# A table of places for preparation, constants and second stage of a fused block-sparse attention and long-convolution kernel

## The chip, the cores and the metric

One Trainium2 chip, one core. The metric is device time in microseconds (us), the median of several runs. The engines are PE (TensorE: matrix products; PEld its weight loads), DVE (VectorE), ACT (ScalarE), POOL (GpSimd) and SP (SyncE, which here only issues DMAs). Each works through its own queue in order and waits for semaphores of the others.

## What is computed

For 4 batches and 8 heads of 768 positions and 64 dimensions, causal attention over the best blocks: each query scores the means of the 12 key blocks of 64, keeps the top three and its own block, and attends to these alone. The heads side by side give x (4 x 768 x 512), which goes through a gated long convolution.

```
k_rep = k.reshape(B, H, n_blocks, 64, D).mean(axis=3)
gate = where(causal, einsum('bhsd,bhnd->bhsn', q, k_rep), -1e9)
mask = (top 3 blocks of gate, or own block) & causal
attn = softmax(where(mask, scale * q @ k.T, -1e9)) @ v
x = heads of attn side by side
x1, x2, x3 = split(x @ w_proj, 3)
x2c = irfft(rfft(x2, axis=1) * rfft(filter_fft, axis=0), axis=1)
out = (x1 * x2c * x3) @ w_out
```

## The kernel before, in words

**Pairs, groups, slots.** Two heads are a pair p (16 pairs, four in a batch). Each head's causal triangle is cut into three groups (`groups`, L390). A slot n is one group of one head: 96 slots, six a pair, 24 a batch. Pair p's slots begin at n0 = 6p. A slot (the loop at L700) issues, in program order: `scores(n+1)` (L400, three products into one of two PSUM tiles `sps`, tag `sc`), `exponentials(n)` (L412, one ACT instruction of 896 columns, then a causal cut on POOL), `flush()` (L600, DMAs and other steps put into `late`), the steps of `early[n]`, one step of the second stage, the constants of `fills[n]`, `products(n-1)` (L423, seven products of the exponentials with V into the one PSUM tile `o`; after a head's last group DVE divides into `xnat`, L445 and L446), more steps of the second stage, and the steps of `bank[n]`. The order written is the order in which each engine executes.

**Preparation of a pair** runs some ten slots ahead. `load` (L74) brings k, q, v. `prep_k` (L289) turns half a pair's k on PE (`turned_pair`, L282), casts it on ACT (L298) and sums its blocks on DVE (L301); at the second half two DMAs send it to KA and KB (L307). `prep_q` (L325) turns q, casts it to TQ (L333, ACT), keeps the rest in `ql` (L335, DVE) and sends the second head to QB (L339). `prep_kr` (L314) forms block means on POOL, `prep_gate` (L341) is sixteen small products, `prep_mask` (L354) ten maxima and two DVE operations, `prep_turn` (L367) turns the mask on PE and copies it (two direct copies for pairs 0 and 1; for later pairs one ACT copy to `m16` and two DMAs from SP). `prep_v` (L310) casts v on POOL. The loop at L647 gives each pair the same slots relative to n0, with exceptions for pairs 1 and 2.

**Second stage** (`hyena`, L478), a batch behind the attention. `turn_x` (L459) or a transposing DMA (L455) brings x to `xT`, `fold` (L471, DVE) makes sums and differences `xf`. Then six `x2` (P steps), six `fft` (F), eight `gates` (X, two PSUM tiles each), four `inverse` (I) and six `output` (O). The step's name in the change carries its numbers: X12 is `gates(dc=2, hf=1)`, F10 is `fft(j=0, which=1)`. `final` (L522) multiplies gate and inverse into `yT` on POOL (in the tail the second half on DVE, L529). A list gives the order, and a credit per slot (costs of 0.65 to 1.28 a step, L703 to L729) says when the next step is issued. In the last batch (`spread` false) the steps run after the slots, with their PSUM in the two `sps` tiles (L481).

**PSUM.** Tag `one` has three tiles in rotation, which kt, qt, g, mt, xt, and in the slots x2p, xx, x1p, x3p, ye, yo, op share; `o` has one.

**Prologue** (L606 to L630): constants, preparation of pair 0, the sine products of the transform's constants, warm products (`warm`, L89: products of a zero tile, 512 columns each, whose result nobody reads), the first scores. **Tail** (L730 to L748): the outputs of batch 2 that are left, warm products, `turn_x`, two gates, `fold`, and the last batch's list.

Of the kernel before, what the change touches and what calls it, by code (L numbers as in the profile page):

```python
# [14 lines left out]
AX = mybir.AxisListType  # L15


@with_exitstack
def kernel(
# [10 lines left out]
    nc = tc.nc  # L30
# [58 lines left out]
    def warm(n):  # L89
        t = ps.tile([P, 512], FP32, name="warm", tag="o", bufs=1)  # L90
        for i in range(n):
            nc.tensor.matmul(t, lhsT=zeros[:, 0:P], rhs=zeros, start=True, stop=True,  # L92
                             skip_group_check=True)

    warm(3)
# [25 lines left out]
    def sine_products(i):  # L121
        if i != 1:
# [3 lines left out]
                         skip_group_check=True)  # L126
        ka = hy.tile([P, F], FP32, name="dft_ka", tag=f"t{i % 2 + 1}", bufs=3)
# [9 lines left out]
    def sine_rest(i):  # L137
        pr, kw = sine.pop(i)
        nc.tensor.matmul(pr, lhsT=idn, rhs=kw, start=False, stop=True, skip_group_check=True)
        nc.scalar.activation(FS[:, i, :], pr, AF.Sin, bias=0.0, scale=TWO_PI / S2)  # L140
# [4 lines left out]
    warm(3)  # L145
# [24 lines left out]
    TQ = [const.tile([P, S], fp, name=f"TQ{i}") for i in range(2)]  # L170
# [118 lines left out]
    def prep_k(p, t):  # L289
        kn = nats["k", p]  # L290
        kh = KH[p % 2]
        if t == 0:
            state["krs", p] = small.tile([P, NB], FP32, name="krs", tag="krs")
        krs = state["krs", p]
        kt = turned_pair("kt", kn, t)

        def cast():
            nc.scalar.copy(kh[:, F * t:F * (t + 1)], kt)  # L298

        def sums():  # L300
            nc.vector.tensor_reduce(out=krs[:, 6 * t:6 * t + 6],  # L301
                                    in_=kt.rearrange("p (n j) -> p n j", j=64),
                                    axis=AX.X, op=ALU.add)
        cast()
        sums()
        if t == 1:
            late.append(lambda: (nc.sync.dma_start(KA[p % 2][0:D, :], kh[0:D, :]),  # L307
                                 nc.sync.dma_start(KB[p % 3][0:D, :], kh[D:P, :])))
# [16 lines left out]
    def prep_q(p, t):  # L325
        qn = nats["q", p]
        tq = TQ[p % 2]
        if t == 0:
            state["ql", p] = hp.tile([P, S], fp, name="ql", tag="ql")
        ql = state["ql", p]  # L330
        qt = turned_pair("qt", qn, t)
        cols = slice(F * t, F * (t + 1))
        nc.scalar.activation(tq[:, cols], qt, AF.Copy, bias=0.0, scale=QS)  # L333
# [4 lines left out]
        if t == 1:  # L338
            late.append(lambda: nc.sync.dma_start(QB[p % 2][0:D, :], tq[D:P, :]))  # L339

    def prep_gate(p):  # L341
        tq, ql, kr = TQ[p % 2], state.pop(("ql", p)), state.pop(("kr", p))
# [24 lines left out]
    def prep_turn(p):  # L367
        mn, tq, qb = MN[p % 2], TQ[p % 2], QB[p % 2]
        mt = one("mt", (P, SC, P), fp)
        for c in range(SC):  # L370
            nc.tensor.transpose(mt[:, c, :], mn[:, c, :], id16)  # L371
        if p < 2:
            flat = mt.rearrange("p c s -> p (c s)")
# [7 lines left out]
        else:  # L381
            m16 = hp.tile([P, S], fp, name="m16", tag="m16")
            nc.scalar.activation(m16[64:108, :], mt[64:108].rearrange("p c s -> p (c s)"),  # L383
                                 AF.Copy, bias=0.0, scale=MQ)
            late.append(lambda: (nc.sync.dma_start(tq[64:64 + NB, :], m16[64:64 + NB, :]),
                                 nc.sync.dma_start(qb[64:64 + NB, :], m16[96:96 + NB, :])))
# [13 lines left out]
    def scores(n):  # L400
# [3 lines left out]
        qq = (QB if h else TQ)[p % 2]  # L404
# [20 lines left out]
    def products(n):  # L425
# [7 lines left out]
        first = g == 0  # L433
        for kc, q0, q1, col in groups[g][0]:
# [5 lines left out]
        if g == NS - 1:  # L440
# [8 lines left out]
            if h == 1:  # L449
# [3 lines left out]
                xT, xf = xTs[b], xTs["f", b]  # L453
                if p >= DC and dc < DC - 1:
                    late.append(lambda: nc.sync.dma_start_transpose(  # L455
                        xT[:, dc, :].rearrange("p (c s) -> p c s", s=P),
                        xn.rearrange("p c s -> p (c s)")))
# [20 lines left out]
    def hyena(b, spread):  # L478
# [8 lines left out]
        def x2(eo, i):  # L487
# [9 lines left out]
            (nc.scalar.copy if eo == 0 or not spread else nc.vector.tensor_copy)(st["x2"][:, eo, i, :], pa)  # L497
# [4 lines left out]
        def fft(j, which):  # L502
# [12 lines left out]
            else:  # L515
# [4 lines left out]
                nc.gpsimd.tensor_add(PQ[:, 1, j, :], tb, t4)  # L520
# [11 lines left out]
        def inverse(dc):  # L532
# [11 lines left out]
            yy = hy.tile([P, 2, F], FP32, name="yy", tag="yy", bufs=DC)  # L544
# [33 lines left out]
        x2s = [(0.85, lambda i=i, e=e: x2(e, i)) for e in range(2) for i in range(HC)]  # L578
        X = lambda dc, hf: (1.28, lambda: gates(dc, hf))
        Fh = lambda j, w: (0.65, lambda: fft(j, w))  # L580
        I = lambda dc: (0.96, lambda: inverse(dc))
        O = [(0.85, lambda i=i: output(i)) for i in range(SC)]
        if spread:
            steps = x2s + [X(0, 0), Fh(0, 0), Fh(0, 1), X(1, 0), Fh(1, 0), Fh(1, 1), X(2, 0),
                           Fh(2, 0), Fh(2, 1), X(3, 0), X(0, 1),
                           I(0), X(1, 1), I(1), X(2, 1), I(2), X(3, 1), I(3)] + O
        else:
            steps = [X(0, 0), X(1, 0)] + x2s[:4] + [
# [28 lines left out]
    for i in range(HC):  # L617
        sine_rest(i)
# [160 lines left out]
```

## Time and profile before

| | |
|---|---|
| time, median of 3 runs | 272.51 us (271.26 to 272.61) |
| the profiled execution's own time | 272.46 us |
| its span, first to last instruction | 270.7 us |
| mean granted TensorE clock | 0.979 |
| HBM read, written | 24.64 MB, 6.29 MB |

The profile is one execution. A row of the timeline is: start, duration (of the whole group if several), engine, line, operation, tiles written and read with their shape, count, and in brackets the idle time of the engine before it with what ended it. A row of the stages is: the stretch and its length, then for each engine the busy time and the count of instructions, the clock that PE was granted, the share of the 16 DMA engines (over 1 means that transfers overlap on an engine), and GB/s. A row of the waits is: who waited for whom, us in total, times, longest. In a row of groups the last numbers are busy us and mean ns of one.

### The profile page before, as it was taken

The page shows a single profiled execution, that of the slowest core. Times are in us where ns is not written, and L with a number is a line of the kernel's source. Part 1 is how long each engine was busy: PE and PEld are TensorE (multiplying, and loading weights), DVE is VectorE, ACT ScalarE, POOL GpSimd, SP SyncE. Part 2 cuts the span into 40 slices and gives each one's busy share as a digit, 9 for nine tenths or more (in the row PEclk, how much of TensorE's full clock was granted, in tenths as well). Part 3 has the DMA queues.
Part 4 walks back from the last instruction along what each step waited for, and adds up shares of the span by engine and source line. Part 5 has one row for each costly group of instructions (what it writes and reads, how often), then busy time and mean ns, then how long its engine had stood idle before and what let it go on. Part 6 is the DMA issues. An engine that isn't in the chain of part 4 may idle for free.

```text
span 270.7 us, 6236 instructions
## 1 busy us (share of the span) xinstructions
PE 242.0 (89%) x2228; PEld 150.3 (56%) x2228; DVE 179.1 (66%) x550; ACT 171.4 (63%) x275; POOL 140.9 (52%) x260
## 2 busy tenths in 40 slices
PE   7696869996999999989999999899999989897874
PEld 3365735565665667655656676566655654443431
DVE  3568658889477988654569885725698663256680
ACT  4567766774767577769764777797756756342333
POOL 7513342689635778653236876714277872006540
PEclk9999979997699999999999999999999999999999
DMA  8997977889797855677665467767241044200006
GB/s 162 209 153 208 245 205 140 157 162 212 128 190 159 155 124 131 125 210 232 150 134 121 106 150 105 190 212 195 59 93 37 1 33 155 77 2 0 0 0 232
DMA packets 93654, 36.29 MB, mean 134 GB/s; under 512 B 84292, under 2 KB 89784, under 8 KB 93624
## 3 DMA queue, kind: packets, MB, share of 16 engines
q1 hardware_dynamic: 91368, 33.81, 54.9%
q0 software_dynamic: 2256, 2.10, 5.9%
q8 instruction: 17, 0.28, 0.5%
q14 instruction: 13, 0.11, 0.2%
HBM read 24.64 MB, written 6.29 MB: 114 GB/s over the span
## 4 chain that ended last, share of the span: by engine, by line
PE 58%; DVE 15%; ACT 10%; POOL 6%; issue 4%; DMA 3%; SPq 1%; POOLq 0%; DVEq 0%; ACTq 0%
PE sps L407 8%; PE x2p L495 7%; PE op L572 6%; PE o L437 5%; PE x3p L560 5%; ACT ex L416 5%; PE x1p L557 4%; PE mt L371 2%; PE kt L285 2%; PE qt L285 2%; PE warm L92 2%; PE sps L557 2%; DVE xnat L446 2%; PE sps L560 2%; PE g L350 2%
## 5 line engine op out<-in xcount | busy, mean ns | idle before, releaser
L416 ACT ACTIVATE ex<-sps 128x896 f16<-128x896 f32 x96 | 88.3, 926 | 3.3 <-PE sps L407 3.0
L419 POOL TENSOR_SCALAR_AFFINE_SELECT ex<-ex 128x256 f16<-128x256 f16 x96 | 40.4, 424 | 82.6 <-ACT ex L416 78.3
L437 PEld LDWEIGHTS <-ex 128*128 128x128 f16 x672 | 32.7, 99 | 26.3 <-DVE xnat L446 11.6
L437 PE MATMUL o<-V,ex 128*128 128x65 f16 x672 | 37.5, 196 | 5.8 <-DVE xnat L446 4.4
L407 PE MATMUL sps<-QB,KB 76*128 76x512 f16 (+1 forms) x144 | 27.0, 297 | 3.7 <-ACT ex L416 3.6
L407 PE MATMUL sps<-TQ,KA 76*128 76x512 f16 (+1 forms) x144 | 27.4, 302 | 1.9 <-DMA QB<-m 1.3
L518 POOL TENSOR_TENSOR PQ<-ta 128x512 f16<-128x512 f32 x12 | 15.2, 1270 | 23.8 <-DVE ta L517 23.8
L572 PE MATMUL op<-wo,yT 128*128 128x512 f16 x96 | 24.2, 379 | 3.0 <-POOL yT L527 3.0
L301 DVE TENSOR_REDUCE krs<-kt 128x6 f32<-128x384 f32 x32 | 17.5, 553 | 13.5 <-ACT KH L298 13.3
L495 PE MATMUL x2p<-wp,xf 128*128 128x512 f16 x96 | 24.3, 379 | 0.8 <-DVE xf L474 0.8
L298 ACT CAST KH<-kt 128x384 f16<-128x384 f32 x32 | 15.2, 481 | 13.9 <-PE kt L285 12.6
L333 ACT ACTIVATE TQ<-qt 128x384 f16<-128x384 f32 x32 | 15.7, 495 | 12.3 <-PE qt L285 12.1
L335 DVE SCALAR_TENSOR_TENSOR ql<-qt,TQ 128x256 f16<-128x256 f32 (+1 forms) x32 | 15.5, 485 | 11.7 <-ACT TQ L333 11.6
L565 DVE TENSOR_TENSOR gg<-x1sb,x3p 128x384 f32<-128x384 f16 x24 | 13.2, 551 | 12.7 <-ACT x1sb L563 7.9
L527 POOL TENSOR_TENSOR yT<-gg,yy 128x384 f16<-128x384 f32 x16 | 15.9, 997 | 10.4 <-DVE yy L545 10.3
L575 ACT COPY osb<-op 128x512 f32<-128x512 f32 x24 | 14.1, 587 | 10.8 <-PE op L572 9.2
L560 PE MATMUL x3p<-xT,wp 128*128 128x384 f16 x96 | 19.6, 326 | 0.5 <-DVE yy L546 0.5
L407 PEld LDWEIGHTS <-KB 76*128 76x128 f16 x144 | 13.6, 100 | 11.0 <-issue 5.6
L557 PE MATMUL x1p<-xT,wp 128*128 128x384 f16 x96 | 19.5, 326 | 0.0
L383 ACT ACTIVATE m<-mt 44x768 f16<-44x768 f16 x14 | 11.3, 805 | 12.6 <-PE mt L371 12.6
L446 DVE TENSOR_TENSOR xnat<-o,rc 128x384 f16<-128x384 f32 x32 | 17.8, 558 | 1.1
L359 DVE MAX8 m<-g 128x8 f32<-128x12 f32 x160 | 13.9, 161 | 6.8 <-PE g L350 6.8
(155 smaller groups left out, 498.0 us busy)
## 6 DMA issues: line engine op xcount, KB each, us to landing
q_nat<-in_q_dram SPq DMA_DIRECT2D x32, 192.0 KB
k_nat<-in_k_dram SPq DMA_DIRECT2D x32, 192.0 KB
v_nat<-in_v_dram SPq DMA_DIRECT2D x32, 192.0 KB
out_dram<-osb SPq DMA_DIRECT2D x24, 256.0 KB
QB<-TQ SPq DMA_DIRECT2D x16, 96.0 KB
KA<-KH SPq DMA_DIRECT2D x16, 96.0 KB
KB<-KH SPq DMA_DIRECT2D x16, 96.0 KB
wp<-in_moe_w_proj_dram POOLq DMA_DIRECT2D x12, 128.0 KB, 3.8
```

The costliest lines, as they stand in the source:

```text
L301: nc.vector.tensor_reduce(out=krs[:, 6 * t:6 * t + 6], in_=kt.rearrange("p (n j) -> p n j", j=64), axis=AX.X, op=ALU.add)
L333: nc.scalar.activation(tq[:, cols], qt, AF.Copy, bias=0.0, scale=QS)
L407: nc.tensor.matmul(t[:, col:col + q1 - q0], lhsT=kk[0:64 + NB, P * kc:P * (kc + 1)], rhs=qq[0:64 + NB, q0:q1], start=True, stop=True, skip ...
L416: nc.scalar.activation(ex, t[:, 0:W], AF.Exp, bias=0.0, scale=EXPS)
L419: nc.gpsimd.affine_select(out=tri, in_=tri, compare_op=ALU.is_ge, fill=0.0, base=0, pattern=[[0, 2], [1, P]], channel_multiplier=-1)
L437: nc.tensor.matmul(o[:, qc, :], lhsT=ex[:, c0:c0 + P], rhs=V16[p % 3][:, kc, h, 0:65], start=first, stop=False, skip_group_check=True)
L446: nc.vector.tensor_tensor(xn[:, :, D * h:D * (h + 1)], o[:, :, 0:D], rc.to_broadcast([P, SC, D]), op=ALU.mult)
L495: nc.tensor.matmul(pa, lhsT=xf[:, eo, dc, P * i:P * (i + 1)], rhs=wp[:, dc, Dm:2 * Dm], start=(dc == 0), stop=(dc == DC - 1))
L527: nc.gpsimd.tensor_mul(st["yT"][:, dc, 0:F], g, yy[:, 0, :])
L557: nc.tensor.matmul(x1p, lhsT=wp[:, d2, dsl], rhs=xT[:, d2, hs], start=(d2 == 0), stop=(d2 == DC - 1))
L560: nc.tensor.matmul(x3p, lhsT=wp[:, d2, 2 * Dm + P * dc:2 * Dm + P * (dc + 1)], rhs=xT[:, d2, hs], start=(d2 == 0), stop=(d2 == DC - 1))
L572: nc.tensor.matmul(op, lhsT=st["yT"][:, cc, P * i:P * (i + 1)], rhs=wo[:, cc, :], start=(cc == 0), stop=(cc == DC - 1))
```

## The change

All orders move into one table, `ORDER`. Each slot has seven places: 0 before `scores(n+1)`, 1 after the exponentials and before `flush`, 2 to 4 after it and before `products(n-1)`, 5 and 6 behind the products. A time is 7 x slot + place; a pair's times count from its n0, and are given for p modulo 4, or for a pair by itself. The preparation is split into steps with a time each: turn, cast and sums of k; turn, copy and rest of q; each DMA of its own; gate; maxima; turn, copy and DMA of the mask. The second stage's steps have a time in the table `mid` (two batches) or `last`, and the tail a list. `zeros` puts products of a zero tile, 256 columns, ahead of `products(n)` of the slots named; they add zero to `o`.

Besides: TQ has three buffers instead of two; masks of pairs from 2 on turn and copy five of six blocks, the first is cleared once; `yy` has three buffers instead of four; warm products in the prologue have 128 columns; the sine products are issued without ACT's step between them and their second half ahead of the gate; in the tail the fold stands ahead of the gates, and one of the additions into PQ is on DVE. A second way to turn q (`cast_q`, `split_q`, `send_q`) is there for pairs from `turned` = 16 on, which is none.

```diff
+ORDER = {
+    "ldk:0": -120, "ldq:0": -84, "ldv:0": -61, "k0:0": -77, "k1:0": -64, "kc0:0": -76, "ks0:0": -76,
+    "kc1:0": -62, "ks1:0": -64, "kd:0": -61, "q0:0": -57, "q1:0": -53, "qc0:0": -57, "qr0:0": -57,
+    "qc1:0": -50, "qr1:0": -50, "qd:0": -45, "kr:0": -54, "g:0": -43, "m:0": -39, "mt:0": -29,
+    "mc:0": -26, "md:0": -26, "v:0": -23, "x:0": 52, "f:0": 69, "ldk:1": -118, "ldq:1": -93,
+    "ldv:1": -57, "k0:1": -77, "k1:1": -71, "kc0:1": -76, "ks0:1": -76, "kc1:1": -64, "ks1:1": -61,
...
+    "ldv:2": -54, ... "kd:2": -51, "q0:2": -59, "q1:2": -50, "qc0:2": -52, "qr0:2": -51,
...
+    "wp20": 156, "wp21": 177, "wp22": 195, "wp23": 215,
+    "w0": 8, "w1": 12, "w2": 0, "w3": 2, "w4": 14, "w5": 0, "turned": 16,
+    "mid": [("P00", 30), ("P01", 31), ("P02", 38), ("P10", 43), ("P12", 47), ("P11", 50),
+        ("F00", 57), ("X00", 57), ("F10", 73), ("F01", 79), ("X01", 82), ("F11", 87), ("X03",
+        89), ("F02", 94), ("F12", 99), ("X11", 103), ("X02", 106), ("I1", 114), ("X10", 120),
+        ("I0", 130), ("I3", 130), ("I2", 136), ("X13", 151), ("X12", 158), ("O0", 163), ("O4",
+        171), ("O3", 177), ("O5", 178), ("O1", 185), ("O2", 194)],
+    "last": [("P00", 31), ... ("I3", 146), ("X12", 147), ("O1", 153), ("O0",
+        157), ("O4", 158), ("O3", 164), ("O2", 167)],
+    "tail": ["rO5", "x", "w2", "w0", "f", "X00", "X01", "P00", "P02", "P01", "P10", "F02",
+        "P11", "F00", "F01", "P12", "F10", "w4", "w1", "F11", "X03", "F12", "X10", "w2", "X11",
+        "X02", "I0", "X12", "I1", "I3", "w2", "w0", "I2", "w1", "X13", "O0", "w1", "O5", "O3",
+        "O1", "O4", "O2"],
+    "dve": ["P10", "P11", "P12"],
+    "zeros": {31: 1, 16: 1, 19: 1, 9: 4, 33: 3, 8: 2, 22: 1, 24: 1, 17: 3, 21: 2, 20: 1, 5: 3,
+        12: 1, 6: 1},
+}
...
+    def turn_k(p, t):
+        if t == 0:
+            state["krs", p] = small.tile([P, NB], FP32, name="krs", tag="krs")
+        state["kt", p, t] = turned_pair("kt", nats["k", p], t), 2
+
+    def cast_k(p, t):
+        nc.scalar.copy(KH[p % 2][:, F * t:F * (t + 1)], taken("kt", p, t))
...
+    def send_mask(p):
+        nc.sync.dma_start(TQ[p % 3][64:64 + NB, :], M16[p % 2][64:64 + NB, :])
+        nc.sync.dma_start(QB[p % 2][64:64 + NB, :], M16[p % 2][96:96 + NB, :])
...
+        for i in range(ORDER["zeros"].get(n, 0)):
+            nc.tensor.matmul(o.rearrange("p c d -> p (c d)")[:, 0:256], lhsT=zeros[:, 0:P],
+                             rhs=zeros[:, 0:256], start=first, stop=False, skip_group_check=True)
+            first = False
...
-                nc.gpsimd.tensor_add(PQ[:, 1, j, :], tb, t4)
+                (nc.vector if j == HC - 1 and not spread else nc.gpsimd).tensor_add(
+                    PQ[:, 1, j, :], tb, t4)
...
+    warm(ORDER["w3"])
     prep_kr(0)
     prep_gate(0)
     prep_mask(0)
-    for i in range(HC):
-        sine_rest(i)
-    nc.scalar.preload_act_table_set("natural_log_exp_and_others")
     mask_rows()
     for p, w in ((2, "k"), (1, "v"), (2, "q")):
         load(p, w)
-    warm(4)
-    prep_turn(0)
-    warm(2)
+    warm(ORDER["w4"])
+    turn_mask(0)
+    copy_mask(0)
...
     for n in range(slots):
+        def do(*places):
+            for i in places:
+                for f in work[n][i]:
+                    f()
+        do(0)
         if n + 1 < slots:
             scores(n + 1)
         exponentials(n)
+        do(1)
         flush()
+        do(2, 3, 4)
         if n:
             products(n - 1)
+        do(5, 6)
```

In `tail`, "rO5" is the one output of batch 2 that is left, "x" the turn of the last pair, "f" its fold, and "w2" two warm products of 512 columns.

More of the change, by code (lines that the diff above doesn't have):

```diff
@@ L144 @@
         sine_products(i)
-    warm(3)
+    for i in range(HC):
+        sine_rounded(i)
     idn = const.tile([P, P], fp, name="idn")
@@ L633, in buffer_rows @@
         nc.sync.dma_start(t[64:64 + NB, :], erow)
[L636 to L652 removed]
+    per = slots // B
@@ L699 @@
-    credit = 0.0
-    for n in range(slots):
-        b, m = divmod(n, per)
+        for i in range(3):
+            once[f"wp{i}{dc}"] = lambda dc=dc, i=i: load_wp(i, dc)
+    for name, f in once.items():
+        at(ORDER[name], f)
+    for b in range(1, B):
+        steps = hyena(b - 1, True)
+        for name, time in ORDER["last" if b == B - 1 else "mid"]:
+            at(7 * per * b + time, steps.pop(name))
+        rest = steps
+    for n in range(slots):
+        def do(*places):
[3 more added lines that the diff above has]
+        do(0)
```

307 lines of the change are left out of this document (154 added, 153 removed), and 31 rows, old and new, of the table ORDER.

## The prediction

> **What bounds the kernel now.** I read the page's head first, then the busy time of each engine by stage (columns: PE, PEld, DVE, ACT, POOL busy, granted clock, DMA share, GB/s). The cuts are the first exponential, the slots of the four batches (24 slots each), and the tail after the last exponential.
>
> ```profile
> span 270.7 us, 6236 instructions
> PE 242.0 (89%) x2228; PEld 150.3 (56%) x2228; DVE 179.1 (66%) x550; ACT 171.4 (63%) x275; POOL 140.9 (52%) x260
> ...
> 0.00:16.70 16.70, 12.70 (x56) 6.24 (x57) 7.74 (x49) 7.47 (x14) 8.86 (x30) 1.00 1.14 192
> 16.70:62.00 45.30, 37.76 (x441) 26.26 (x440) 34.96 (x121) 33.34 (x52) 22.29 (x51) 0.96 0.82 178
> 62.00:118.10 56.10, 52.88 (x533) 35.23 (x533) 41.99 (x125) 37.82 (x61) 38.85 (x69) 0.94 0.79 155
> 118.10:173.70 55.60, 53.36 (x543) 34.68 (x540) 38.66 (x120) 40.32 (x67) 30.69 (x56) 1.00 0.65 150
> 173.70:226.60 52.90, 50.56 (x480) 31.13 (x477) 34.77 (x100) 36.65 (x59) 28.38 (x47) 1.00 0.41 97
> 226.60:270.70 44.10, 34.72 (x190) 16.70 (x188) 20.94 (x37) 15.75 (x30) 11.87 (x11) 0.99 0.17 65
> ```
>
> The mean of 89% hides four regimes. From 62 to 226.6 us the tensor engine is the bound: idle 3.2, 2.2 and 2.3 us in the three stages, so an order can win little there. The first batch leaves PE idle 7.5 of 45.3 us. The tail leaves 9.4 of 44.1. Before 16.7 us no attention slot runs, and the DMA engines are full (share above 1). Gain has to come from the front, the first batch and the tail. A slot lasts 55.60/24 = 2.3 us.
>
> **The change part by part.** The sum goes against the profiled execution's own time, 272.46 us (span 270.7 and 1.8 around it); the median of 272.51 is the same within 0.05.
>
> *1. Prologue.* The warm products (products of a zero tile that only keep PE going) shrink from 512 to 128 columns, the sine products go ahead of the gate, the mask's turn follows the gate and 14 warm products.
>
> ```profile
> 4.46 1.46 PE L92 MATMUL warm<-zeros 128*128 128x512 f16 x3
> ...
> 5.71 1.49 PE L285 MATMUL qt<-id,q_nat 128*128 128x128 f32 x6
> ...
> 12.16 0.22 DVE L365 TENSOR_TENSOR MN<-lt,ownm 128x120 f16<-128x120 f16 x1
> 12.43 1.91 PE L92 MATMUL warm<-zeros 128*128 128x512 f16 x4
> 14.13 0.85 PE L371 MATMUL mt<-id,MN 128*128 128x128 f16 x6
> 15.02 0.56 DVE L377 TENSOR_SCALAR TQ<-mt 12x768 f16<-12x768 f16 x1 [2.64 <-PE mt L371]
> 15.72 1.62 PE L407 MATMUL sps<-TQ,KA 76*128 76x512 f16 x6
> ...
> 16.66 0.92 ACT L416 ACTIVATE ex<-sps 128x896 f16<-128x896 f32 x1 [2.14 <-PE sps L407]
> ```
>
> The mask is ready at 12.38 and its turn starts at 14.13: four warm products of about 0.43 us stand between, 1.7 us on the path that sets the first exponential. In the table the 14 small ones follow the gate directly: 14 x 0.43/4 = 1.5 us, from about 10.8 to 12.3, so they lie beside the maxima. The first warm products also end earlier (12 x 0.11 = 1.3 us after the sine products, which no longer wait for ACT between them), so the turn of q can leave up to 0.8 us sooner. At most 1.7 + 0.8 = 2.5, at least 0. What is late next is k: the DMA that puts its cast into KA queues behind ten loads of 192 KB, 1.97 MB at some 217 GB/s, 9 us, with DMA full:
>
> ```profile
> 7.20:10.65 3.45, 1.87 (x19) 1.35 (x19) 2.56 (x7) 1.45 (x3) 2.87 (x8) 1.00 1.39 219
> 10.65:14.06 3.41, 2.83 (x17) 1.07 (x14) 1.37 (x12) 2.18 (x4) 0.41 (x1) 1.00 1.22 200
> ```
>
> By this estimate k cannot be there long before 13, and scores not long before 13.5, so I take **-2.0**.
>
> *2. Zero products, 25 of 256 columns, in fourteen slots from 6 to 34.* They aim at the clock. Stretches just before and in the two drops:
>
> ```profile
> 34.20:37.70 3.50, 1.66 (x17) 1.04 (x17) 3.13 (x9) 2.99 (x5) 2.43 (x7) 0.99 0.69 202
> 37.70:41.10 3.40, 3.40 (x30) 1.84 (x29) 1.06 (x2) 0.92 (x1) 0.75 (x2) 0.51 0.82 198
> ...
> 58.10:61.50 3.40, 3.10 (x29) 1.84 (x29) 2.85 (x8) 2.63 (x6) 3.08 (x5) 1.00 0.46 105
> 61.50:65.00 3.50, 1.88 (x31) 1.45 (x30) 3.16 (x15) 1.41 (x3) 3.33 (x8) 0.99 1.01 224
> 65.00:68.40 3.40, 2.95 (x26) 2.12 (x24) 3.21 (x8) 1.66 (x3) 3.38 (x6) 0.50 1.23 224
> 68.40:71.80 3.40, 3.39 (x27) 2.61 (x25) 1.83 (x6) 2.66 (x4) 1.64 (x5) 0.50 0.60 80
> ```
>
> Each drop follows a stretch with PE busy about half (1.66 and 1.88 of 3.5 us). The six zeros of slots 9 and 10 add 6 x 0.107 = 0.64 us to the first; 0.107 is half of 0.215 a product, which the 21 products of the tail's last row (part 4) give. Those of slots 20 to 25 add some 0.7 to the second. In the drops PE was busy 3.40 + 2.95 + 3.39 = 9.74 us at half speed: full speed saves at most 4.9. If nothing is saved and no zero falls in a wait, they cost 25 x 0.107 = 2.7. DVE is as full as PE in 65.00:68.40, so half of the saving stays behind it: -2.4, and of the zeros 0.4 on the path, since most fall where PE idles: **-2.0**.
>
> The Trainium skill, "TensorE: Matmul & The Clock Gate", section "Why this matters for your kernels", asks only that no PE idle gap exceed about 3 us, since one idle window lowers the clock. This trace disagrees: the clock fell after stretches with 17 and 31 products in 3.5 us. By the Trainium skill's page nothing would be there to hold, and the sum would lose this term (a rival below).
>
> *3. Slots.* The tables `mid` and `last` keep the work per slot and move the inverse ahead: in `mid` the last I stands at 136 (slot 19) and the first O at 163 (slot 23). Before, O(0) followed I(3) by one slot and waited for POOL's yT:
>
> ```profile
> PE op L572 <- POOL yT L527: 3.0, 4, 0.9
> ...
> 117.22 0.39 PE L572 MATMUL op<-wo,yT 128*128 128x512 f16 x1 [0.83 <-POOL yT L527]
> ...
> 122.53 0.50 PE L371 MATMUL mt<-id,MN 128*128 128x128 f16 x6
> ```
>
> Two of the four waits go: -1.7. In `last`, O1 (153) still follows I3 (146) by a slot: its wait stays. Masks of pairs 2 to 15 turn five blocks instead of six: 14 x about 0.055 = -0.8; the ACT copy shortens too, where ACT has room (63%). Against it, the load wp2 of block 3 is issued on POOL at 215 (slot 30, before: 29) and the first gates need it at slot 32:
>
> ```profile
> wp<-in_moe_w_proj_dram POOLq DMA_DIRECT2D x12, 128.0 KB, 3.8
> ...
> 81.26 0.65 PE x1p L557 x4
> ```
>
> Ten places of seven per slot are 1.4 x 2.3 = 3.3 us for a landing of 3.8 behind POOL's own waits; all of PE's queue stands behind the gates. Between 0 and 2 us; I take +0.5. DMA issues keep their order on SP but for neighbours (v's loads ahead of KA and KB in every fourth pair), whose users come six slots later: 0, with cover of some 14 us; were it gone, a load's 0.9 us. Holding casts and sums apart from the turns: 0, its other end is the slower rival. Slots: **-2.0** (bounds -4 and +12).
>
> *4. Tail.*
>
> ```profile
> 228.15 1.89 PE L572 MATMUL op<-wo,yT 128*128 128x512 f16 x8
> ...
> 228.59 0.56 DVE L446 TENSOR_TENSOR xnat<-o,rc 128x384 f16<-128x384 f32 x1
> ...
> 230.31 0.50 PE L467 MATMUL xt<-id,xnat 128*128 128x128 f16 x6
> 230.65 1.03 PE L92 MATMUL warm<-zeros 128*128 128x512 f16 x4
> ...
> 235.77 2.98 PE L495 MATMUL x2p<-wp,xf 128*128 128x512 f16 x13 [0.85 <-DVE xf L474]
> ...
> 255.69 1.06 DVE L529 TENSOR_TENSOR yT<-gg,yy 128x384 f16<-128x384 f32 x1
> ...
> 257.73 0.66 PE L537 MATMUL sps<-IC,PQ 128*128 128x384 f16 x3 [0.87 <-DVE yy L546]
> ...
> 259.69 0.82 PE L557 MATMUL sps<-xT,wp 128*128 128x384 f16 x4 [0.80 <-DVE yy L546]
> ...
> 262.25 4.71 PE L572 MATMUL op<-wo,yT 128*128 128x512 f16 x21 [0.44 <-POOL yT L527]
> ```
>
> The last row gives a product of 512 columns: 4.71 us for 21, about 0.215 apart beside the last one's drain. xnat is ready at 229.15, but its turn waits behind two outputs until 230.31. With one output left (rO5) it can go at 229.2: -1.1; the other output moves into the slots, where a wait covers half of its 0.86: +0.4. Two warm products fewer: -0.2 beside that. The fold now precedes the gates on DVE, so the 0.85 us wait of the first x2 goes: -0.85. With X12 and X13 between the inverses, two waits of 0.8 are half covered: -0.8. One PQ add moves from POOL to DVE, unseen there:
>
> ```profile
> L519 DVE TENSOR_TENSOR tb<-xx,Asb 128x512 f32<-128x512 f32 x6 | 4.1, 681 | 0.0
> ```
>
> Between 0.7 (this row) and 1.3 (yT's 1.0 us scaled from 384 to 512); half of 0.9 delays what follows: +0.5. The 11 warm products, 11 x 0.215 = 2.4 us, fit the 9.4 us idle: 0, without that cover 2.4. **-2.0** (bounds -5 and +2).
>
> Sum: 272.46 - 2.0 - 2.0 - 2.0 - 2.0 = 264.5 us.
>
> **The rivals.**
> *Data sets the front* (268.5). DMA's share of 1.14 before and 0.82 in the first batch speaks for it: slots that start sooner wait for k, q and the filter, and terms 1 and 2 vanish: 264.5 + 4.0. Against it: in 16.70:62.00 DMA still has a fifth free.
> *The zeros do not hold the clock* (266.9): the drop has another cause than PE's share, or its window moves with the start; 264.5 + 2.4. That is also what the rule of the Trainium skill's page on TensorE gives.
> *More idle closes* (257.5). PE idles 7.5 + 3.2 + 2.2 + 2.3 = 15.3 us in the slots; if the 300 separate places close half, 5.5 us go beyond what term 3 took, and 1.5 in the tail. Against it: DVE's 34.96 of 45.30 us.
> *Banks held longer: slower* (276.5). All turns, gates and hyena steps share three PSUM banks (tag `one`). The table releases them later: g at -43 and its maxima at -39, q's turn at -59 and its rest at -51, k's at -71 and its sums at -61. A step that needs two banks then stops PE. The precedent:
>
> ```profile
> PE g L344 <- DVE hsb L260: 0.9, 1, 0.9
> ```
>
> At 1 us for each of the twelve pairs prepared in the full stages that is +12. It decides from 8.0/12 = 0.7 us a pair. Against it: only one such wait in the trace, and most holds stay within a slot.
>
> **How the numbers follow.** Forecast 264.5: 0.45. Data sets the front: 0.20. Zeros fail: 0.08. More idle closes: 0.10. Banks: 0.13. Gains and losses that cancel: 0.04. A measurement tells 0.5% (1.4 us) from no change. Faster by more than that: the first four, less 0.04 of the front's spread that ends near 272: 0.79. Within: 0.07. Slower: 0.14, the banks and a little of the cancelling case. The range runs from the wide gain to just short of no change, 257.0 to 272.0, leaving out the banks and half of the cancelling.
>
> **What would show it.** Term 1: the first ex at 14.4 to 15 instead of 16.66, mt right behind MN. Term 2: no half-clock stretch between 30 and 75 us, with stretches of 3.4 us there above 2 us busy. Term 3: no wait of op for yT but in the last batch; the full stage at 54 to 55 us. Term 4: from the last ex's start to the end 42 instead of 44.1 us. It would be wrong if PE waits for releases of `one` tiles by DVE or ACT in every pair, if the first ex comes sooner but batch 0 grows by as much, or if the first half-speed stretch lasts a window longer.

## The result, and the profile after

| | before | after |
|---|---|---|
| median | 272.08 us (4 runs, 271.26 to 272.61) | 258.63 us (4 runs, 257.25 to 259.04) |
| the profiled execution, its span | 272.46, 270.7 us | 258.57, 256.9 us |

The ratio is 0.950, 95% interval 0.945 to 0.954: 13.4 us faster, where 8.0 were forecast. The page's head and the stages of the changed kernel, cut as before at the first exponential, the batches of 24 slots, and the start of the last exponential:

```profile
span 256.9 us, 6293 instructions
PE 238.7 (93%) x2270; PEld 153.6 (60%) x2270; DVE 182.8 (71%) x551; ACT 169.9 (66%) x275; POOL 139.8 (54%) x261
...
0.00:14.20 14.20, 10.61 (x80) 7.57 (x81) 8.13 (x49) 7.13 (x14) 8.83 (x30) 0.95 1.11 189
14.20:58.60 44.40, 40.07 (x467) 29.61 (x465) 36.75 (x122) 33.16 (x51) 24.10 (x58) 0.94 0.95 194
58.60:111.90 53.30, 49.80 (x525) 33.42 (x526) 42.08 (x124) 37.52 (x62) 36.97 (x64) 1.00 0.92 162
111.90:164.30 52.40, 52.32 (x537) 34.53 (x534) 38.66 (x120) 39.97 (x67) 30.62 (x55) 1.00 0.76 159
164.30:215.20 50.90, 49.77 (x474) 31.02 (x471) 35.33 (x100) 36.33 (x58) 28.27 (x47) 1.00 0.41 101
215.20:256.90 41.70, 36.15 (x198) 17.44 (x196) 21.86 (x38) 15.76 (x30) 11.05 (x10) 1.00 0.19 70
```

Stage by stage against before: the prologue 14.2 for 16.7 us, the first batch 44.4 for 45.3, the second 53.3 for 56.1, the third 52.4 for 55.6, the fourth 50.9 for 52.9, the tail 41.7 for 44.1. So 8.0 of the 13.8 us come from the three stages of which the prediction said that an order could win little there, since PE was idle only 2 to 3 us in each. Read the third stage: PE is now busy 52.32 of 52.40 us. It does not only lose its idle time (2.2 us before); its busy time falls too, from 53.36 to 52.32 us, with 6 products fewer in the trace. What PE waited for in that stage before (PE's own rows of the list of waits between 118.1 and 173.7 us; the last numbers are us, times, longest):

```profile
PE op L572 <- POOL yT L527: 0.8, 1, 0.8
PE sps L407 <- ACT ex L416: 0.6, 1, 0.6
PE o L437 <- DVE xnat L446: 0.5, 1, 0.5
PE x3p L560 <- DVE yy L546: 0.2, 1, 0.2
```

In the changed kernel the same list, between 111.9 and 164.3 us, has no row of PE at all. The prologue, in the timeline of the changed kernel:

```profile
10.11 0.94 PE L150 MATMUL warm<-zeros 128*128 128x128 f16 x14
...
11.52 0.22 DVE L455 TENSOR_TENSOR MN<-lt,ownm 128x120 f16<-128x120 f16 x1
11.80 0.45 PE L465 MATMUL mt<-id,MN 128*128 128x128 f16 x5 [0.69 <-DVE MN L455]
12.55 0.56 DVE L474 TENSOR_SCALAR TQL<-mt 12x768 f16<-12x768 f16 x1 [0.80 <-DMA QB<-TQL]
...
13.25 1.65 PE L504 MATMUL sps<-TQL,KA 76*128 76x512 f16 x6 [1.00 <-DVE TQL L474]
...
14.19 0.92 ACT L513 ACTIVATE ex<-sps 128x896 f16<-128x896 f32 x1 [2.66 <-PE sps L504]
```

The mask's turn starts 0.06 us after the mask is there (1.75 before), and the first exponential at 14.19 instead of 16.66 us. The scores then wait 1.00 us for DVE's copy of the mask into TQL, which the trace puts behind the DMA from TQL to QB; no wait for k stands there.

### The profile page after: what moved, and what is told of

Same layout as the page of the kernel before. It is cut to its first block, busy times and chain, and to the rows that moved or that the text cites. A ratio compares the mean times of both kernels' runs of the same rounds, so it can differ in the third digit from the quotient of the medians.

```text
span 256.9 us, 6293 instructions
## 1 busy us (share of the span) xinstructions
PE 238.7 (93%) x2270; PEld 153.6 (60%) x2270; DVE 182.8 (71%) x551; ACT 169.9 (66%) x275; POOL 139.8 (54%) x261
## 4 chain that ended last, share of the span: by engine, by line
PE 69%; DVE 13%; DMA 8%; ACT 4%; issue 3%; POOL 1%; SPq 1%; ACTq 0%; DVEq 0%
PE sps L504 11%; PE op L675 8%; PE x2p L596 7%; PE o L538 6%; PE x3p L663 6%; PE x1p L660 5%; PE kt L354 4%; PE qt L354 3%; DMA TQL<-M 3%; PE xx L609 3%; DMA xT<-xnat 2%; PE ye L640 2%; PE sps L660 2%; PE yo L643 2%; PE g L440 2%
## 5 line engine op out<-in xcount | busy, mean ns | idle before, releaser
L538 PE MATMUL o<-V,ex 128*128 128x65 f16 x672 | 36.8, 194 | 2.5 <-POOL ex L516 1.4
L504 PE MATMUL sps<-TQL,KA 76*128 76x512 f16 (+1 forms) x144 | 27.1, 300 | 1.8 <-DVE TQL L474 1.0
L408 DVE SCALAR_TENSOR_TENSOR TQL<-qt,TQL 128x256 f16<-128x256 f32 (+1 forms) x32 | 15.4, 486 | 14.1 <-ACT TQL L403 13.9
L403 ACT ACTIVATE TQL<-qt 128x384 f16<-128x384 f32 x32 | 15.4, 494 | 11.2 <-PE qt L354 10.9
L371 ACT CAST KH<-kt 128x384 f16<-128x384 f32 x32 | 15.5, 483 | 9.1 <-DVE krs L374 4.5
L660 PE MATMUL x1p<-xT,wp 128*128 128x384 f16 x96 | 19.5, 326 | 0.2 <-DVE tb L621 0.2
L663 PE MATMUL x3p<-xT,wp 128*128 128x384 f16 x96 | 19.5, 326 | 0.1
L354 PE MATMUL qt<-id,q_nat 128*128 128x128 f32 x96 | 17.8, 300 | 1.2 <-DMA q_nat<-in_q_dram 1.0
L666 ACT CAST x1sb<-x1p 128x384 f16<-128x384 f32 x24 | 11.5, 480 | 10.5 <-PE x1p L660 10.4
L504 PEld LDWEIGHTS <-KA 76*128 76x128 f16 x144 | 12.8, 99 | 9.1 <-issue 3.8
```

Of the source, the lines that this page charges most:

```text
L354: nc.tensor.transpose(y[:, P * c:P * (c + 1)], x[:, HC * t + c].rearrange("p h d -> p (h d)"), id32)
L504: nc.tensor.matmul(t[:, col:col + q1 - q0], lhsT=kk[0:64 + NB, P * kc:P * (kc + 1)], rhs=qq[0:64 + NB, q0:q1], start=True, stop=True, skip ...
L538: nc.tensor.matmul(o[:, qc, :], lhsT=ex[:, c0:c0 + P], rhs=V16[p % 3][:, kc, h, 0:65], start=first, stop=False, skip_group_check=True)
L660: nc.tensor.matmul(x1p, lhsT=wp[:, d2, dsl], rhs=xT[:, d2, hs], start=(d2 == 0), stop=(d2 == DC - 1))
L663: nc.tensor.matmul(x3p, lhsT=wp[:, d2, 2 * Dm + P * dc:2 * Dm + P * (dc + 1)], rhs=xT[:, d2, hs], start=(d2 == 0), stop=(d2 == DC - 1))
```

## The experiments

In each, the kernel is the changed one with one edit. Times are medians; the plain difference is against the 258.63 us above, and each ratio is to the kernel before on the same chip. The intervals reach 0.005 to 0.010 to either side, which is 1.4 to 2.7 us, and the ratios put all edits but tail_old 0.2 to 2.6 us further from the changed kernel than the plain differences do (prologue_old 2.7 us by ratio, 1.3 by difference). So a difference under about 2 us in this table is told only where a profile shows where it comes from. The third stage (slots 48 to 71) is the cleanest to read, because it is repeated work without loads of constants; its length is given between the starts of the 49th and the 73rd exponential of the profiled execution.

| edit | time, us | ratio to before (95%) | third stage, us |
|---|---|---|---|
| none | 258.63 | 0.950 (0.945 to 0.954) | 52.40 |
| zeros0 | 258.94 | 0.952 (0.946 to 0.957) | 52.40 |
| prep_old | 264.39 | 0.972 (0.967 to 0.978) | 54.59 |
| stage2_old | 265.97 | 0.979 (0.973 to 0.986) | 55.67 |
| both_old | 267.77 | 0.985 (0.981 to 0.990) | 55.31 |
| coupled | 265.39 | 0.982 (0.975 to 0.990) | 54.62 |
| act_coupled | 263.43 | 0.971 (0.966 to 0.976) | 54.62 |
| dve_coupled | 262.72 | 0.969 (0.964 to 0.974) | 53.41 |
| six_blocks | 258.73 | 0.954 (0.949 to 0.959) | 52.66 |
| prologue_old | 259.94 | 0.960 (0.953 to 0.967) | 52.39 |
| tail_old | 261.64 | 0.960 (0.951 to 0.970) | 52.40 |
| better | 262.04 | 0.972 (0.962 to 0.982) | 52.40 |
| wp_late | 259.31 | 0.955 (0.949 to 0.962) | 52.39 |

**zeros0** leaves out the products of zero tiles.

```diff
+ORDER["zeros"] = {}
```

> The changed kernel without its 25 zero products (they add nothing to the result). Clock theory of the prediction: the share of PE's work decides the clock, so one or two half-speed stretches of 3.4 us come back between 30 and 75 us from the start, where the changed kernel has none, and the time goes from 258.6 to about 260.6 (259.6 to 263). Rival, from the rule that only an idle window lowers the clock: nothing to hold, no new half-speed stretch, 258.2 to 258.6.

Measured: 0.3 us more, inside what a measurement can tell, so the price that the clock theory gave, 2.0 us, is not borne out. Its half-speed stretch does come back, which the rival denied (the stages of this kernel: stretch, length, busy times, then granted clock, DMA share, GB/s):

```profile
57.00:60.40 3.40, 1.73 (x30) 1.26 (x31) 2.03 (x3) 1.01 (x2) 2.52 (x5) 1.00 0.36 75
60.40:63.80 3.40, 3.40 (x33) 2.70 (x30) 3.16 (x16) 2.28 (x4) 2.36 (x5) 0.51 1.25 225
```

But the first two batches together take 97.88 us without the zeros and 97.68 with them. DMA is above 1 and DVE busy 3.16 of 3.40 us in that stretch; that a PE at full speed would have waited there for part of the time fits this, but is argued. Nor do the zeros hold the clock for certain: of the eleven other edited kernels, all of which keep them, nine show a half-speed stretch that begins between 55 and 66 us, six_blocks (below) among them:

```profile
58.40:61.80 3.40, 2.20 (x39) 1.58 (x36) 3.29 (x16) 2.46 (x4) 3.37 (x6) 1.00 1.01 202
61.80:65.20 3.40, 3.40 (x34) 2.94 (x32) 2.26 (x4) 2.35 (x3) 2.81 (x6) 0.50 1.22 229
```

Its first two batches take 96.74 us, less than those of the changed kernel, which has no such stretch. The clock's fall there costs nothing that these runs can tell. That does not hold for every fall: of the ten executions of both_old (below), the three with a mean granted clock of 0.991 or more took 265.05 to 267.81 us, the other seven (0.985 or less) 266.44 to 268.62; and of the four of the changed kernel the fastest (257.25 us) has the highest clock, 0.997, and the slowest (259.04) the lowest, 0.980. In zeros0 no such order is seen. Clock and time may have a common cause there; no run separates them.

**prep_old, stage2_old, both_old** put the old relative places of the preparation, the old list of the second stage, or both into the new loop.

```diff
+for _c in range(4):
+    ORDER.update({f"{n}:{_c}": t for n, t in {
+        "ldk": -117, ... "k0": -78, "kc0": -78, "ks0": -78, ... "g": -43, "m": -43, "mt": -29, "mc": -29,
...
+_old = ["P00 P01", "P02", "P10", "P11 P12", "X00", "F00", "F10 X01", "F01", "F11 X02", "F02", "F12 X03"]
+_mid = _old + ["X10", "I0", "X11", "I1", "X12", "I2", "X13", "I3", "O0", "O1 O2", "O3", "O4 O5"]
```

> The changed kernel with the preparation's steps (k, q, gate, mask, v, their loads and DMAs, turn and fold of x) at the places that the kernel before gave them; second stage, constants, zeros, prologue and tail stay. In the full stages the change gained 8.0 us. Theory 'preparation': casts and sums put behind the exponentials and apart from their turns made most of it, so 5 to 7 us come back: 264 to 266. Rival 'second stage': its step table made it, so 258.6 to 260.5 here.

> The changed kernel with the second stage's steps in the slots in the order and slots of the kernel before (two outputs left for the tail instead of one); preparation, zeros, prologue and the rest of the tail stay. Theory 'second stage': 5 to 7 us come back, 264 to 266, with PE idle 2 us again in the full stage of batch 2. Rival 'preparation': only the wait of the first output for yT returns, twice 0.8, and the output's 0.9 in the tail: 260 to 261.5.

> The changed kernel with both of the last two edits at once: the preparation's steps and the second stage's steps at the places of the kernel before; zeros, prologue and the rest of the tail stay. Alone the first cost 5.8 us and the second 7.3 us. Theory 'the two tables are fitted to each other': together they cost little more than the second alone, 265 to 267.5, and the full stage of batch 2 takes 55.6 us as in the kernel before. Rival 'each table has its own gain': the costs add up, 258.6 + 5.8 + 7.3 = 271.7 (270 to 273).

Measured: 5.8, 7.3 and 9.1 us more. Both theories of the first two runs got the 5 to 7 us that they asked for, so neither table is the cause by itself. 9.1 is well below 5.8 + 7.3 = 13.1: the costs do not add up, as the theory of fitted tables said (its upper end, 267.5, was missed by 0.3). The waits of PE in the third stage show where they overlap. First the kernel with the old preparation, then the one with the old second stage:

```profile
PE sps L518 <- ACT ex L527: 1.2, 2, 0.8
PE mt L479 <- ACT yes L660: 0.2, 1, 0.2
```

```profile
PE op L681 <- POOL yT L636: 0.8, 1, 0.8
PE sps L510 <- ACT ex L519: 0.6, 1, 0.6
PE o L544 <- DVE xnat L553: 0.5, 1, 0.5
...
```

The old list brings back three waits of before one for one (and one of 0.2 us for a copy of an output). The old preparation brings others, of the scores for an exponential and of the mask's turn for a copy of the second stage. With both old, the rows of the kernel before stand there (0.8 for yT, 0.6 for ex, 0.5 for xnat, 0.2 for yy), and not the sum of the two: either table beside the other's old order has waits of its own. With both old the third stage takes 55.31 us, and before, between the same two exponentials, 55.56; the 0.25 us between them is what the mask blocks give (six_blocks below). So in this stage nothing is left for the buffers of TQ and yy, which were not tried by themselves; whether the new places could do without them stays open.

**coupled, act_coupled, dve_coupled** keep all places but give a cast, sum, copy or maximum the place of the turn (or gate) that it reads: for all of them, for ACT's alone, or for DVE's alone.

```diff
+for _k in list(ORDER):
+    for _a, _b in (("k0", "kc0"), ("k1", "kc1"), ("q0", "qc0"), ("q1", "qc1"), ("mt", "mc")):
+        if _k[:len(_a) + 1] in (_a + ":", _a + "."):
+            ORDER[_b + _k[len(_a):]] = ORDER[_k]
```

This is ACT's; DVE's has ("k0", "ks0"), ("k1", "ks1"), ("qc0", "qr0"), ("qc1", "qr1"), ("g", "m").

> The changed kernel, but each cast, sum, rest of q, maxima and mask copy stands at the same place as the turn or gate that it reads, as in the kernel before; turns, loads, DMAs and all other places stay. Theory 'the separation is what the preparation's table gains': most of prep_old's 5.8 us come back, 262.5 to 265. Rival 'the places of loads, DMAs, v, x and the first pairs are': 258.6 to 260.5. Under the prediction's slower rival (banks held longer) this would even be faster than 258.6.

> As after, but ACT's casts of k and q and its copies of the mask share the place of their turns again; DVE's sums, rests and maxima keep their own places. Theory (ACT's casts, placed ahead of the next exponential, wait for PE's turn and make the exponential late, which frees sps late): most of what coupling all of them cost (6.6 us) is here, 262.5 to 266 us, the stage of slots 48 to 71 at 53.8 to 54.6 us instead of 52.4, and waits of PE's scores for ACT's exponential back. Rival (it is DVE's steps that hold the banks of tag one): 258.5 to 260.5 us, stage at 52.4 to 52.8.

> As after, but DVE's sums of k share the place of the turn, its rest of q that of the cast, its maxima that of the gate; ACT's casts and copies keep their places. Theory (ACT is the engine that matters): 258.5 to 260.5 us, stage of slots 48 to 71 within 0.4 us of 52.4. Rival (DVE's steps matter): 262 to 265 us, stage above 53.4 us, and PE waits for DVE in it.

Measured: 6.8, 4.8 and 4.1 us more (6.8, where the second expectation has 6.6); coupled lies 0.4 us above its forecast, and is slower where the rival of held banks would have had it faster. In the third stage the theory that ACT's places matter holds: they alone give the whole 54.62 us. In the sum of all stages it falls, and for DVE's places the rival came true: they cost nearly as much, 1.0 us in the third stage and 2.3 in the first two batches together. There the first is 3.7 us longer (48.14 us for 44.42) and the second 1.4 shorter (51.88 for 53.26). The mechanism of ACT's part, in the timeline of act_coupled:

```profile
159.49 0.70 ACT L483 ACTIVATE M<-mt 44x640 f16<-44x640 f16 x1 [0.53 <-PE mt L469]
...
160.22 0.48 ACT L375 CAST KH<-kt 128x384 f16<-128x384 f32 x1
...
160.59 1.73 ACT L517 ACTIVATE ex<-sps 128x896 f16<-128x896 f32 x2
...
161.56 0.38 PE L508 MATMUL sps<-QB,KB 76*128 76x512 f16 x1 [1.18 <-ACT ex L517]
```

and the same slot of the changed kernel:

```profile
156.46 0.92 ACT L513 ACTIVATE ex<-sps 128x896 f16<-128x896 f32 x1
...
157.41 0.70 ACT L479 ACTIVATE M<-mt 44x640 f16<-44x640 f16 x1
...
157.83 0.55 PE L504 MATMUL sps<-QB,KB 76*128 76x512 f16 x3
...
158.13 0.48 ACT L371 CAST KH<-kt 128x384 f16<-128x384 f32 x1
...
158.51 0.92 ACT L513 ACTIVATE ex<-sps 128x896 f16<-128x896 f32 x1
```

With its turn's place the mask's copy stands ahead of an exponential, waits 0.53 us for PE, and takes 0.70; a cast follows with 0.48. The exponential comes that much later, two then run back to back, and PE, which has only two tiles `sps`, waits 1.18 us for one. In the table an exponential goes ahead of that copy, and nobody waits. DVE's part has the same form (timeline of dve_coupled, then PE's waits in its third stage, and in its first batch):

```profile
158.94 0.55 DVE L378 TENSOR_REDUCE krs<-kt 128x6 f32<-128x384 f32 x1
...
159.52 0.48 ACT L375 CAST KH<-kt 128x384 f16<-128x384 f32 x1 [1.43 <-DVE krs L378]
```

```profile
PE mt L469 <- ACT KH L375: 0.6, 1, 0.6
```

```profile
PE qt L358 <- DMA q_nat<-in_q_dram: 3.4, 1, 3.4
```

In the third stage DVE's sum of kt comes first and ACT, idle for 1.43 us, casts the same tile only behind it; the next turn on PE waits for that cast. In the first batch the largest wait is for a load of q, 3.4 us for 1.0. SP's part of the timeline, in dve_coupled and in the changed kernel:

```profile
47.58 3.98 SPq L139 DMA_DIRECT2D q_nat<-in_q_dram  x2
```

```profile
46.46 2.77 SPq L135 DMA_DIRECT2D q_nat<-in_q_dram  x2
```

SP begins the load 1.1 us later and takes 1.2 us longer to issue it. It is the load of pair 5, and the same two numbers go together in two other runs below: SP takes 1.36 us for it in wp_late, where PE does not wait for it, and 3.55 in better, where PE waits 3.7. What in DVE's places delays it is not settled.

**six_blocks** turns and copies all six blocks of each mask again.

```diff
-        for c in range(0 if p < DIRECT else 1, SC):
+        for c in range(SC):
...
-            nc.scalar.activation(M16[p % 2][64:108, P:S], flat[64:108, P:S], AF.Copy, bias=0.0, scale=MQ)
+            nc.scalar.activation(M16[p % 2][64:108, :], flat[64:108, :], AF.Copy, bias=0.0, scale=MQ)
```

> As after, but the masks of pairs 2 to 15 turn and copy all six blocks again. By the prediction's term of 0.055 us a block: 14 more on PE, 0.8 us: 259.4 us, each full stage 0.2 us longer. Rival 1 (hidden beside DVE and ACT): 258.6 us, stages as in after. Rival 2 (the table is fitted to these lengths and breaks): over 261 us, with new waits in the full stages.

Measured: the third stage is 0.26 us longer and the fourth 0.23, as the theory's 4 x 0.055 us a stage gives. In the time it is 0.1 us, below what can be told, so there the forecast of 0.8 is neither shown nor refuted.

**prologue_old** has the warm products of 512 columns and the old order of sine products, gate and mask.

```diff
-    warm(ORDER["w4"])
+    warm(4, 512)
     turn_mask(0)
     copy_mask(0)
-    warm(ORDER["w5"])
+    warm(2, 512)
```

> The changed kernel with the prologue as before (warm products of 512 columns, four of them between gate and turn of the mask, sine products interleaved with ACT and behind the maxima, cast ahead of the sums). Theory of the prediction: the first exponential comes at about 16.7 instead of 14.2 us and the time follows one to one, 260.6 to 261.5. Rival 'data sets the front': the first batch makes up for it, 258.6 to 259.6.

Measured: the first exponential 1.2 us later (15.42, where 16.7 was expected), the time 1.3 us longer, between the theory's range and the rival's. The first two batches together do not make up for it (98.01 us for 97.68), so the front pays one to one, as far as differences of this size can be told: the first exponentials of the kernels whose prologue is the changed one spread from 13.96 to 14.75 us.

Half of the 2.5 us comes from these edits. Most of the other half is PE's speed in the two traces. The four warm products of 512 columns start at 11.77 us here and the mask's turn at 12.89, 1.12 us; before, the same four took 1.70 (12.43 to 14.13). The three sine products, with their wait for ACT, take 1.24 us here and 1.68 before. Together that is 1.0 us for the same instructions. Another 0.2 us is the gate, which starts that much earlier: here, as in the changed kernel, the sums stand ahead of the casts, and the edit does not undo that, though the expectation says so.

**tail_old** has the old order of the tail.

```diff
+ORDER["tail"] = ("rO5 w2 x w4 X00 X01 f P00 P01 P02 P10 F00 P11 F01 P12 F02 X02 F10 X03 F11 X10 F12 "
+                 "X11 X12 I0 I1 I2 I3 X13 O0 O1 O2 O3 O4 O5").split()
```

> The changed kernel with the order of the tail as before (one output left instead of two). The prediction's terms for the tail's order: two warm products ahead of the turn 0.4, the fold behind two gates 0.85, waits of the inverses 0.8, so about 2 us come back: 260.6 (259.6 to 261.5). Rival: the tail gained only because it starts with one output fewer and DVE takes an addition, so 258.6 to 259.2.

Measured: 3.0 us more (four executions, 258.72 to 262.41), and in the profiled execution 2.2 us from the start of the last exponential to the end:

```profile
215.40:259.30 43.90, 34.80 (x191) 16.66 (x189) 22.12 (x38) 15.85 (x30) 10.63 (x10) 0.99 0.18 66
```

PE is busy 1.35 us less than in the changed kernel's last stage, with 7 products fewer, all warm ones, and the stage is still longer, by 2.2 us. The waits are back: PE waits 0.8 us for the fold, 1.7 for the gates' tile `gg` (0.9 in the changed kernel), 2.3 for DVE behind the inverses (0.4) and 0.4 for yT. The rival, that the order of the tail gains nothing, does not fit; the time is 0.1 us above the theory's range.

**better and wp_late** look for a faster kernel. The first brings forward the load of q in every fourth pair, copies pair 2's mask directly, and has more warm products; the second issues six loads of projection weights two to four slots later.

```diff
+ORDER.update({"ldq:0": -98, "w4": 24, "w5": 12})
...
+ORDER.update({"wp11": 130, "wp10": 139, "wp12": 146, "wp13": 153, "wp00": 162, "wp20": 172})
```

> The changed kernel with three more edits: pair 2's mask is copied directly on DVE instead of through two DMAs (scores waited 0.6 us for them in slot 11), q of every fourth pair is loaded two slots earlier (-98 instead of -84; its turn waited 1.0 us for the load in slot 21), and 22 more small warm products stand around the first mask's turn, where PE waits, to keep full speed in the first slots (half speed from 12.6 to 19.5 us now). If waits for data and clock set the first batch, 256 to 257.5. If DVE sets it (36.75 of 44.40 us busy), 258 to 259.5.

> As after, but the six first loads of the projection (128 KB each, issued by POOL in slots 15 to 24, 4 to 5 us each to land) are issued two to four slots later. Theory (in batch 0 the DMA engines set the pace: the load of q that slot 21 waits 1.0 us for shares them with these loads): that wait shrinks below 0.5 us and batch 0 takes 43.2 to 44.0 us instead of 44.42; of this 0 to 1 us is lost again where the loads now meet the transfers of slots 22 to 28: 257.5 to 259 us. Rival (the wait of slot 21 comes from SP issuing that load late, behind DMAs that wait): it stays at 0.8 us or more and batch 0 within 0.3 us of 44.4. Other end: the first x2 steps wait for their weights in slot 28, batch 1 is 2 us longer, 260 to 261 us.

Measured: 3.4 us more, above both ranges, and 0.7 more, which is no difference. PE's waits in the first batch, of the changed kernel, of better, and of wp_late:

```profile
PE qt L354 <- DMA q_nat<-in_q_dram: 1.0, 1, 1.0
...
PE sps L504 <- DMA TQL<-M: 0.6, 1, 0.6
```

```profile
PE qt L355 <- DMA q_nat<-in_q_dram: 3.7, 1, 3.7
PE sps L505 <- DMA KB<-KA: 1.6, 1, 1.6
```

```profile
PE sps L505 <- DMA TQL<-M: 1.8, 1, 1.8
...
PE sps L505 <- DMA KB<-KA: 0.9, 1, 0.9
```

In better the edit misses the wait that it was made for. It brings forward the loads of pairs 4, 8 and 12, but the turn that waits in slot 21 is that of pair 5, and now waits 3.7 us; why the kernel is slower by 3.4 us is not settled. In wp_late the wait for q is gone, as the theory of the shared DMA engines said, but the stage is not shorter, 45.3 us, and no step of x2 waits for its weights. Its longer waits for a mask and for KB come in slots 8 and 11, ahead of the edit, so they are not its doing. They show how far one profile of this stage can be trusted: tail_old and stage2_old issue the same work up to slot 28, and their first batches took 44.33 and 45.61 us. No run was faster than the changed kernel.

## Why the prediction came out as it did

The direction was right. The sum was 5.4 us short. By the stages of the two profiles the slots gave 8.9 us, where terms 2 and 3 had 4.0; prologue and tail were 0.5 and 0.4 short. The shortfall would have been larger if term 2 had not been too high: 2.0 us were forecast for the zero products, which gave 0.3, within the noise. That these two errors cancel in part is luck.

**Term 1, prologue** (-2.0): right in size, half of it for the reason given. -2.5 by the first exponential, which the forecast put at 14.4 to 15 and which came at 14.19, with the mask's turn right behind the mask. The edits give 1.2 of it; about 1.0 comes from PE running at full speed, which the term did not have. It read the 0.43 us of a warm product of 512 columns without asking why it is twice the 0.215 of the tail, and priced the 14 small ones at 1.5 us; they took 0.94. Nor is k what is late next: the scores wait for DVE's copy of the mask. The rival that data sets the front is refuted in its main claim, since the first batch did not give the 2.5 us back (44.4 for 45.3). It lives on inside that batch, where DMA's share rose from 0.82 to 0.95.

**Term 2, zero products** (-2.0): wrong. Without them the time is 0.3 us longer. Two steps failed. "Full speed saves at most 4.9", of which half was kept as gain: a half-speed stretch costs nothing here that could be told; PE idles 4.3 and 3.5 us in those two batches and 7.5 and 1.5 without the zeros, so there may be time to take it from. And the zeros are no hold: the changed kernel has no half-speed stretch between 30 and 75 us, as forecast, but nine kernels with the same zeros have one, so that this sign came true is luck. The changed kernel has another in place of those, from about 12.65 to 19.5 us. The rival "the zeros do not hold the clock" was right in its price.

The Trainium skill's rule on idle gaps, "TensorE: Matmul & The Clock Gate", section "Why this matters for your kernels", is not borne out by zeros0 either: its clock fell at 60.4 us after a stretch of 3.40 us in which PE was busy for 1.73, so no gap inside it was longer than 1.67 us, and the page names about 3. (The gap there began ahead of the stretch and lasted 2.45 us in all; in six_blocks the longest one in the 3.4 us ahead of the fall was 0.82.)

**Term 3, slots** (-2.0, with a full stage at 54 to 55 us): this is the term that was mis-sized most. Undoing both tables costs 9.1 us, and the full stage is 52.4. Three steps of it:
- "In `last`, O1 (153) still follows I3 (146) by a slot: its wait stays." All four waits of the outputs for yT are gone, in `last` too.
- "Holding casts and sums apart from the turns: 0". Taken back as a whole it costs 6.8 us, the largest part that was followed to single waits. The prediction judged it by ACT's share of busy time (63%) and by the banks that are held longer. What decides in the third stage is the place in the queue: which of ACT's casts stand ahead of an exponential (2.2 us there), and which of DVE's sums stand ahead of a cast (1.0).
- The late load of wp2's block 3, +0.5: no wait for any load of wp stands in the list of waits of the whole span; 0.

The reading behind all three, that idle PE time of 2 to 3 us is all that a stage can give, was wrong as well. The third stage lost 3.2 us where PE was idle 2.2. Fewer mask blocks explain 0.2 to 0.3 of the rest. The remaining 0.7 us lies in what the profile counts as busy. In this stage prep_old, both_old and the changed kernel all have 537 products in the trace, and PE is busy 53.03, 53.15 and 52.32 us: so the same work counts as less busy time where the waits are gone. That it is the drain of the matmuls ahead of each wait which counts as busy would fit, but is argued.

**Term 4, tail** (-2.0): right, and for the reasons given: tail_old brings their waits back. 41.7 for 44.1 us, forecast 42. The turn of x starts right behind xnat (xnat ends at 217.92), the first x2 products follow the gates without a wait, the two waits of 0.8 us behind the inverses are down to 0.4, and the addition moved to DVE takes what the lower end said, 0.69 us (timeline of the changed kernel):

```profile
217.36 0.56 DVE L547 TENSOR_TENSOR xnat<-o,rc 128x384 f16<-128x384 f32 x1
217.97 0.51 PE L568 MATMUL xt<-id,xnat 128*128 128x128 f16 x6
...
221.35 3.62 PE L596 MATMUL x2p<-wp,xf 128*128 128x512 f16 x16
...
235.36 0.69 DVE L622 TENSOR_TENSOR PQ<-tb 128x512 f16<-128x512 f32 x1
...
242.84 0.65 PE L640 MATMUL sps<-IC,PQ 128*128 128x384 f16 x3 [0.40 <-DVE gg L668]
...
246.01 0.82 PE L660 MATMUL sps<-xT,wp 128*128 128x384 f16 x4 [0.42 <-DVE yy L649]
```

**The rivals.** "More idle closes" (257.5) came nearest, and in part for its reason: PE's idle time in the four stages falls from 15.3 to 9.0 us. But up to 2.7 us of that is filled by the zero products and not closed, by the prediction's 25 x 0.107, and the stages became shorter by 8.9 us, more than the idle time that went. "Banks held longer: slower" did not come about: no wait of PE in the third stage at all, and the kernel that releases them sooner by its places (coupled) is 6.8 us slower.

The pieces add up within what can be told. Zeros 0.3, both tables 9.1, prologue 1.3 and tail 3.0 make 13.7 us, for 13.4 between the medians; that it fits so closely is luck, since by the ratios the same four make about 15.5.

## What to carry to other kernels

When an engine is nearly full, read the waits that remain in its stage and ask, for each, what stands ahead of the releasing instruction in that engine's queue; an engine at 63% can still be late every time it matters. Take one table out alone and the loss counts the misfit with the other as well, so judge two orders fitted to one another by undoing both. Before paying for a full clock, see whether PE has idle time around the slow stretch; here a stretch of 3.4 us at half speed in the second batch cost nothing that could be told, though that does not speak for other places. And compare the duration of the same product in two stretches before trusting a clock column.

## What the runs showed of the hardware

The granted clock does not follow from PE's busy share alone. In the changed kernel these two stretches have the same share:

```profile
9.50:13.00 3.50, 1.98 (x35) 1.55 (x34) 2.01 (x14) 2.02 (x3) 0.94 (x4) 0.95 1.26 208
13.00:16.40 3.40, 3.15 (x14) 2.57 (x15) 2.06 (x13) 1.58 (x3) 0.85 (x3) 0.50 1.39 219
...
60.40:63.80 3.40, 1.96 (x31) 1.42 (x30) 3.17 (x8) 1.96 (x4) 3.37 (x6) 1.00 1.08 212
```

The clock fell in the last tenth of the first (1.98 of 3.50 us) and stayed at full speed through and after the second (1.96 of 3.40). The borders are set by hand, but the prologue shows the same: from 9.20 to 12.65 us PE is busy 2.02 us in the changed kernel, whose clock then falls, and 1.98 in wp_late, which issues the same instructions and keeps a clock of 1.00 to 19.5 us. What it goes by is left open.

The granted clock of the rows does not show half speed at the start of an execution. In the changed kernel fourteen warm products of 128 columns take 0.94 us at 10.11 (shown with the result), and twelve of them, earlier, take longer, both in stretches with a clock of 1.00:

```profile
3.31 1.46 PE L150 MATMUL warm<-zeros 128*128 128x128 f16 x12
```

In the kernel before, four of 512 columns take 1.91 us at 12.43 and 1.03 at 230.65, so there PE was still at half speed where the row says 1.00, and its mean clock of 0.979 is too high.

An addition of 128x512 from fp32 to fp16 takes 0.69 us on DVE (term 4) and 1.27 us on POOL (the groups of the changed kernel):

```profile
L622 POOL TENSOR_TENSOR PQ<-tb 128x512 f16<-128x512 f32 x11 | 14.0, 1270 | 0.0
```
